# The head of a spectral and gated-MLP kernel: x and the first DFT blocks on two DMA queues, mod's first rows read from PSUM

## The chip, the cores and the metric

The kernel runs on one core of a Trainium2 chip. TensorE (PE in the profile; PEld is its weight load) multiplies matrices, VectorE (DVE), ScalarE (ACT) and GpSimd (POOL) work elementwise, and SyncE (SP) issues most of the transfers from HBM. The metric is the device time of one execution in microseconds; lower is better. All times in this text are microseconds unless they say ns.

## The reference

```python
mod = (_silu(c) @ w_mod).reshape(c.shape[0], 6, 1, -1)
sa, ca, ga, sb, cb, gb = (mod[:, 0], mod[:, 1], mod[:, 2], mod[:, 3], mod[:, 4], mod[:, 5])
h = _layernorm(x, axis=-1) * (1 + ca) + sa
x = x + ga * _A_ref(h, A_dft_seq_re, A_dft_seq_im, A_dft_hid_re, A_dft_hid_im)
h = _layernorm(x, axis=-1) * (1 + cb) + sb
x = x + gb * _B_ref(h, B_w_in, B_w_sp, B_b_sp, B_w_out)
```

x is 2048 x 512, `c` is 1 x 512 and `w_mod` 512 x 3072, all float32. `_A_ref` is the real part of a DFT along both axes: `y = Cr @ (h @ Hr.T) - Ci @ (h @ Hi.T)`, where Cr and Ci are the 2048 x 2048 DFT matrices. `_B_ref` is a gated MLP with a 2048 x 2048 spatial weight. The change touches only what happens before the first DFT products.

## The kernel before

The rows of x are handled in 16 tiles of 128 rows, s = 0 to 15, loaded in four groups of four (`load_x`, one buffer `x0` to `x3` per group). The group's 128 partitions are filled by four transfers, each to 32 partitions, called quarters here.

*mod.* Each of mod's six rows is needed on all 128 partitions. `load_mod(j)` loads the four 128 x 512 pieces `wm` of row j. `sum_mod_first(j, ...)` (L222) sums them on TensorE: `scb` holds silu(c) spread over 128 columns, so that `scb.T @ wm` gives the row on every partition, in PSUM (`modp`). `sum_mod` (L211) does some of the pieces on VectorE ahead of it, into `wm[0]`, and TensorE then adds that partial sum with a matrix of ones. ScalarE copies `modp` into SBUF (`keep_mod`, L209). Row 1 is the scale (1 is added), row 0 the shift.

*h.* For a tile, `stats_x` takes mean and variance on VectorE (L87, L89) and 1/std on POOL (L91 to L99), `norm_x` normalizes on ScalarE into `xn` (L103), `scale_x` multiplies with mod 1 (L278) and `shift_x` adds mod 0 (L281). Tiles 0 to 2 do the last two on VectorE, tile 3 in two fused steps (`make_x`, L283), tiles 4 to 15 on POOL. `hi_h` and `lo_h` then split the result into a rounded part `hh` (ScalarE, L296) and the rest `hl` (VectorE, L301).

*DFT blocks.* The DFT matrices come in 512 x 512 blocks, `load(b)`, four quarters each, into `stage` (two buffers). A block serves four steps n = 4b to 4b + 3: `prep_hi(n)` transposes a part on VectorE (`t`, L142) and rounds it on ScalarE (`ah`, L165), `prep_lo(n)` subtracts on VectorE (`al`, L174). `mm_a(n)` is step n of the product `gp`: twelve matmuls, for each of four banks hh with ah, hh with al, hl with ah (L79 to L81). For the first group of 512 rows of the DFT, steps 0 to 3 use x tiles 0 to 3, steps 4 to 7 the same tiles with block 1, steps 8 to 15 tiles 4 to 7, and so on.

*Order.* It is written by hand. Each engine runs its instructions in the order of the program. The lines at L535 to L567 are the head; after it, `at(n, f, ...)` hangs work on step n of the loop that calls `prep(n)`, `mm_a(n)` and `run(n)`. `prep(n)` prepares three steps ahead. Transfers use eight completion semaphores in turn (DMAHW0 to DMAHW7 below), over all queues; an issue whose semaphore is still held by an earlier transfer waits for that one to land, and what stands behind it on the issuing engine waits too. `keep_busy(n, k)` (L232) issues n matmuls on constant data whose result is not used.

Of the kernel before, what the change touches and what calls it, by code (L numbers as in the profile page):

```python
# [8 lines left out]
F32 = mybir.dt.float32  # L9
# [10 lines left out]
def fnet_gmlp_kernel(  # L20
# [107 lines left out]
    NE = 4 * len(src)  # L128
    stage, T, AH, AL = {}, {}, {}, {}

    def load_block(tile_, a):
        v = a.rearrange("(b j) (a s) -> a j b s", j=32, a=4)
        for q in range(4):
            nc.sync.dma_start(tile_[32 * q:32 * q + 32], v[q])

    def load(b):
        if b < len(src):
            stage[b] = blocks.tile([P, 16, P], F32, tag="stage", bufs=2, name=f"stage{b}")
            load_block(stage[b], src[b])

    def squares(dst, block, k):
        nc.vector.transpose(dst.rearrange("p (b i) -> p b i", i=32), block[:, :, 32 * k:32 * k + 32])  # L142
# [50 lines left out]
    nc.scalar.activation(sc, ccol, AF.Silu)  # L193
# [3 lines left out]
    for k in range(ND):  # L197
        nc.vector.tensor_scalar(scb[:, k, :], ones, sc[:, k:k + 1], None, op0=ALU.mult)
    wm, mods = {}, {}

    def load_mod(j):
        wm[j] = [SP[-1].tile([P, D], F32, tag=f"wm{k}", bufs=2 if len(SP) == 1 else 1, name=f"wm{j}_{k}") for k in range(ND)]
        for k in range(ND):
            nc.sync.dma_start(wm[j][k], w_mod[k * P:(k + 1) * P, j * D:(j + 1) * D])

    def keep_mod(j, ps, pl, plus_one):
        if j not in mods:
            mods[j] = pl.tile([P, D], F32, name=f"mod{j}")
        nc.scalar.activation(mods[j], ps, AF.Copy, bias=1.0 if plus_one else 0.0)  # L209
# [9 lines left out]
                    d = mods[j] = pl.tile([P, D], F32, name=f"mod{j}")  # L219
                nc.vector.scalar_tensor_tensor(d, w[k], sc[:, k:k + 1], w[0], op0=ALU.mult, op1=ALU.add)  # L220

    def sum_mod_first(j, k, pl, plus_one, summed=0):  # L222

        ps = bank(k, f"modp{j}")
        w = wm.pop(j)
        for m in range(summed, ND):
            nc.tensor.matmul(ps, scb[:, m, :], w[m], start=m == summed, stop=not summed and m == ND - 1)
        if summed:
            nc.tensor.matmul(ps, ones, w[0], start=False, stop=True)
        keep_mod(j, ps, pl, plus_one)  # L230

    def keep_busy(n, k):  # L232

        ps = bank(k, "busyp")
        for _ in range(n):
            nc.tensor.matmul(ps, ones, busy, start=True, stop=True)
# [19 lines left out]

    X, XG, LN, NRM, h_hi, h_lo = {}, {}, {}, {}, {}, {}

    def load_x(g, ks=range(4)):

        if g not in XG:
            XG[g] = spool.tile([P, 4, D], F32, tag="x", bufs=2, name=f"x{g}")
        k0, k1 = ks[0], ks[-1] + 1
        v = x.rearrange("(g a k i) d -> g a i k d", g=NQ, a=4, i=32)
        for a in range(4):
            nc.sync.dma_start(XG[g][32 * a:32 * a + 32, k0:k1, :], v[g, a][:, k0:k1, :])
        for k in ks:
            X[4 * g + k] = XG[g][:, k, :]

    def stats_x(s):  # L270
        NRM[s] = norm([X[s]], "x")
# [7 lines left out]

    def shift_x(s, eng):  # L280
        eng.tensor_tensor(LN[s], LN[s], mods[0], op=ALU.add)  # L281

    def make_x(s):  # L283

        mean, rstd = stats([X[s]], "x")
        LN[s] = spool.tile([P, D], F32, tag="xn", bufs=4, name=f"xn{s}")
        nc.vector.scalar_tensor_tensor(LN[s], X.pop(s), mean, mods[1], op0=ALU.subtract, op1=ALU.mult)
        nc.vector.scalar_tensor_tensor(LN[s], LN[s], rstd, mods[0], op0=ALU.mult, op1=ALU.add)

    def parts_h(s, t):  # L290

# [263 lines left out]
    shift_x(1, nc.vector)  # L555
    hi_h(1)
    lo_h(0)
    shift_x(2, nc.vector)
    lo_h(1)
    prep_hi(0)  # L560
    prep_lo(0)
    hi_h(2)
    prep_hi(1)
    prep_lo(1)
    lo_h(2)
    make_x(3)
    prep_hi(2)  # L567
    at(0, hi_h, 3)
    at(1, lo_h, 3)
    at(1, load_x, 2)  # L570
# [201 lines left out]
```

## Time and profile before

| | |
|---|---|
| Median of 3 runs (lowest to highest) | 1002.75 (1002.17 to 1003.09) |
| Profiled execution, its own time | 1002.38 |
| Span of the profiled execution | 1000.6 |
| Mean granted TensorE clock | 0.997 |
| First matmul of the DFT product, after the span's start | 19.75 |
| TensorE busy in 0 to 25 / 25 to 50 / 50 to 100 / 100 to 400 | 17.11 / 25.00 / 49.64 / 300.00 |

The profile is of one execution; times in it count from the start of the span. A row of the timeline gives start, duration, engine, line, operation, output <- inputs, and in brackets the idle time ahead of it with what ended it. A row of the waits gives total, times and longest. A row of the windows gives, for a stretch, the busy time of each engine with its count of instructions, then the granted clock as a share of full speed (PEclk), the busy share of the DMA engines and GB/s.

### The profile page before, as it was taken

How to read it: one execution, taken by the hardware profiler on the slowest of the kernel's cores; microseconds unless marked ns; L12 is line 12 of the kernel's file. 1: busy time of each engine (PE TensorE's matmuls, PEld its weight loads, DVE VectorE, ACT ScalarE, POOL GpSimd, SP SyncE). 2: the span in 40 equal slices, each digit the busy share in tenths (PEclk: the TensorE clock that was granted, in tenths of full speed). 3: DMA queues.
4: the chain of work that ended last, by engine and by line, in shares of the span. 5: the costliest groups of instructions: out<-in, count | busy, mean ns of one | idle time of the engine just before them, and what ended most of it. 6: DMA issues, size and time to landing. Idle time of an engine off the chain costs nothing.

```text
span 1000.6 us, 11611 instructions
## 1 busy us (share of the span) xinstructions
PE 988.1 (99%) x4350; PEld 818.3 (82%) x4350; DVE 544.0 (54%) x820; ACT 295.6 (30%) x450; POOL 173.1 (17%) x281
## 2 busy tenths in 40 slices
PE   6999999999999999999999999999999999999998
PEld 3878888888888888888888998888888888888886
DVE  6888864786465646547433676565332622262315
ACT  3444531432132323222533665431111111111101
POOL 2576002022210122004311121102000200020001
PEclk8999999999999999999999999999999999999999
DMA  9786761555355344556553132435225222521141
GB/s 246 154 189 139 156 147 53 150 156 147 85 148 104 90 111 110 112 126 163 195 199 116 43 83 45 116 71 148 66 63 158 53 64 64 158 69 48 42 138 43
DMA packets 145961, 114.28 MB, mean 114 GB/s; under 512 B 7024, under 2 KB 125808, under 8 KB 145904
## 3 DMA queue, kind: packets, MB, share of 16 engines
q1 hardware_dynamic: 139296, 93.61, 39.7%
q0 software_dynamic: 6080, 19.93, 5.5%
q8 instruction: 34, 0.56, 0.2%
q14 instruction: 23, 0.19, 0.1%
q10 hardware_dynamic: 528, 0.00, 0.0%
HBM read 93.59 MB, written 19.92 MB: 113 GB/s over the span
## 4 chain that ended last, share of the span: by engine, by line
PE 51%; DVE 1%; ACT 0%; POOL 0%; issue 0%; ACTq 0%; POOLq 0%
PE gw L79 10%; PE gw L80 10%; PE gw L81 10%; PE z2p L80 3%; PE z2p L81 3%; PE z2p L79 3%; PE op L79 2%; PE op L81 2%; PE op L80 2%; PE z1p L79 2%; PE z1p L80 2%; PE z1p L81 2%; DVE x_last L518 0%; DVE al L174 0%; DVE t L142 0%; ACT L414 0%
## 5 line engine op out<-in xcount | busy, mean ns | idle before, releaser
L174 DVE TENSOR_TENSOR al<-t,ah 128x512 fp32r<-128x512 f32 x224 | 163.0, 728 | 271.0 <-PE gw L80 139.5
L165 ACT ACTIVATE ah<-t 128x512 fp32r<-128x512 f32 x224 | 141.5, 632 | 543.6 <-PE gw L81 212.5
L79 PE MATMUL gp<-ah,hh 128*128 128x512 f32 x512 | 200.9, 392 | 3.7 <-ACT ah L165 3.4
L80 PE MATMUL gp<-al,hh 128*128 128x512 f32 x512 | 200.3, 391 | 0.0
L81 PE MATMUL gp<-ah,hl 128*128 128x512 f32 x512 | 200.3, 391 | 0.0
L81 PE MATMUL gw<-ah,zl 128*128 128x512 f32 x448 | 174.3, 389 | 0.0
L80 PE MATMUL gw<-al,zh 128*128 128x512 f32 x448 | 174.3, 389 | 0.0
L79 PE MATMUL gw<-ah,zh 128*128 128x512 f32 x448 | 174.3, 389 | 0.0
L142 DVE STREAM_TRANSPOSE t<-stage 128x512 f32<-128x512 f32 x208 | 146.0, 703 | 2.8
L79 PEld LDWEIGHTS gp<-ah,hh 128*128 128x128 f32 x512 | 96.8, 189 | 25.2 <-ACT ah L165 4.2
L80 PEld LDWEIGHTS gp<-al,hh 128*128 128x128 f32 x512 | 96.7, 189 | 20.9 <-DVE al L174 0.7
L81 PEld LDWEIGHTS gp<-ah,hl 128*128 128x128 f32 x512 | 96.7, 189 | 20.6 <-DVE hl L301 0.5
L81 PEld LDWEIGHTS gw<-ah,zl 128*128 128x128 f32 x448 | 84.1, 188 | 17.6
L79 PEld LDWEIGHTS gw<-ah,zh 128*128 128x128 f32 x448 | 84.1, 188 | 17.4
L80 PEld LDWEIGHTS gw<-al,zh 128*128 128x128 f32 x448 | 84.1, 188 | 17.3
L496 POOL TENSOR_TENSOR u<-u,g 128x512 f32<-128x512 f32 x16 | 21.5, 1341 | 336.1 <-DVE g L494 336.1
L367 POOL DMA_DIRECT2D x_d<-xr x16 | 8.8, 548 | 246.5 <-DVE xr L366 246.5
L79 PE MATMUL yp<-hth,gh 128*128 128x512 f32 x128 | 49.8, 389 | 0.0
L80 PE MATMUL yp<-htl,gh 128*128 128x512 f32 x128 | 49.8, 389 | 0.0
L81 PE MATMUL yp<-hth,gl 128*128 128x512 f32 x128 | 49.8, 389 | 0.0
L80 PE MATMUL z2p<-wil,ah 128*128 128x448 f32 x128 | 46.7, 365 | 0.0
L79 PE MATMUL z2p<-wih,ah 128*128 128x448 f32 x128 | 46.7, 365 | 0.0
(106 smaller groups left out, 1164.9 us busy)
## 6 DMA issues: line engine op xcount, KB each, us to landing
stage<-in_A_dft_seq_re_dram SPq DMA_DIRECT2D x64, 256.0 KB, 4.9
stage<-in_A_dft_seq_im_dram SPq DMA_DIRECT2D x64, 256.0 KB, 4.8
stage<-in_B_w_sp_dram SPq DMA_DIRECT2D x64, 256.0 KB, 4.8
stage<-h_d SPq DMA_DIRECT2D x32, 256.0 KB, 4.8
z_d<-z POOLq DMA_DIRECT2D x28, 256.0 KB, 5.8
u<-z_d SPq DMA_DIRECT2D x4, 1792.0 KB, 8.2
wm<-in_w_mod_dram SPq DMA_DIRECT2D x24, 256.0 KB, 5.3
xr<-in_A_x_dram POOLq DMA_DIRECT2D x16, 256.0 KB, 3.1
```

The source lines that it names most:

```text
L79: nc.tensor.matmul(acc, ah, bh, start=first, stop=False)
L80: nc.tensor.matmul(acc, ah, bl, start=False, stop=False)
L81: nc.tensor.matmul(acc, al, bh, start=False, stop=last)
L142: nc.vector.transpose(dst.rearrange("p (b i) -> p b i", i=32), block[:, :, 32 * k:32 * k + 32])
L165: nc.scalar.activation(AH[n], T[n], AF.Copy)
L174: nc.vector.tensor_tensor(AL[n], T.pop(n), AH[n].bitcast(F32), op=ALU.subtract)
L367: nc.gpsimd.dma_start(x2_d[t][i * P:(i + 1) * P, :], x2)
L496: eng.tensor_tensor(U[t][:, f, :], U[t][:, f, :], g, op=ALU.mult)
```

## The change

The head is written anew:

- `load_x` and `load` take an engine and a list of quarters. Quarters 0 and 1 of x's first group go out on ScalarE's queue, 2 and 3 on SyncE's; for block 0, block 1 and x's second group, 0 and 1 go out on SyncE's and 2 and 3 on ScalarE's. All four tiles of x's first group are loaded at once (three, then one, before), and go through `stats_x` and `norm_x` alike; `make_x` is gone.
- `make_sc` comes after the first issues.
- mod 1 is summed on TensorE first and stays in PSUM; tiles 0 and 1 are scaled from there in a fused step (add 1, multiply) on VectorE. Tiles 2 and 3 are scaled on POOL from ScalarE's copy.
- mod 0 has two of its pieces summed on VectorE instead of three; tiles 0 and 1 are shifted from PSUM.
- Block 0's first part is prepared right behind tile 0. In step 0, four matmuls with hh and ah come first, then four with hl, then four with al.
- The three idle matmuls ahead of gp are gone, the two at the start become three.
- The shift of tile 3 and `lo_h` of tile 2 hang on step 0.

```diff
+    def load(b, eng=nc.sync, qs=range(4)):
         if b < len(src):
-            stage[b] = blocks.tile([P, 16, P], F32, tag="stage", bufs=2, name=f"stage{b}")
-            load_block(stage[b], src[b])
+            if b not in stage:
+                stage[b] = blocks.tile([P, 16, P], F32, tag="stage", bufs=2, name=f"stage{b}")
+            load_block(stage[b], src[b], eng, qs)
...
+    def make_sc():
+        nc.scalar.activation(sc, ccol, AF.Silu)
+        for k in range(ND):
+            nc.vector.tensor_scalar(scb[:, k, :], ones, sc[:, k:k + 1], None, op0=ALU.mult)
...
-    def sum_mod_first(j, k, pl, plus_one, summed=0):
+    def sum_mod_first(j, k, summed=0):
 
         ps = bank(k, f"modp{j}")
         w = wm.pop(j)
+        if summed:
+            nc.tensor.matmul(ps, scb[:, summed, :], w[summed], start=True, stop=False)
+            nc.tensor.matmul(ps, ones, w[0], start=False, stop=False)
+            summed += 1
         for m in range(summed, ND):
-            nc.tensor.matmul(ps, scb[:, m, :], w[m], start=m == summed, stop=not summed and m == ND - 1)
-        if summed:
-            nc.tensor.matmul(ps, ones, w[0], start=False, stop=True)
-        keep_mod(j, ps, pl, plus_one)
+            nc.tensor.matmul(ps, scb[:, m, :], w[m], start=m == 0, stop=m == ND - 1)
+        return ps
...
+        if n == 0:
+            for a, b in ((h_hi[s], ah), (h_lo[s], ah), (h_hi[s], al)):
+                for k in range(ND):
+                    nc.tensor.matmul(GP[t, j, k], a[:, k, :], b, start=a is h_hi[s] and b is ah, stop=False)
+            return
...
-    load_x(0, range(3))
+    load_x(0, nc.scalar, (0, 1))
+    load_x(0, nc.sync, (2, 3))
     load_mod(1)
+    make_sc()
     load_mod(0)
-    load(0)
-    load_x(0, range(3, 4))
-    load(1)
-    load_x(1)
-    keep_busy(2, 5)
-    for s in range(3):
+    load(0, nc.sync, (0, 1))
+    keep_busy(3, 5)
+    mod1 = sum_mod_first(1, 7)
+    for s in range(4):
         stats_x(s)
-    for s in range(3):
-        norm_x(s)
-    sum_mod(0, range(3))
-    sum_mod_first(1, 7, spool, True)
-    sum_mod_first(0, 6, spool, False, 3)
-    keep_busy(3, 5)
-    for s in range(3):
-        scale_x(s)
-    shift_x(0, nc.vector)
+    sum_mod(0, range(2))
+    norm_x(0)
+    norm_x(1)
+    load(0, nc.scalar, (2, 3))
+    norm_x(2)
+    keep_mod(1, mod1, spool, True)
+    norm_x(3)
+    for s in range(2):
+        nc.vector.scalar_tensor_tensor(LN[s], mod1, 1.0, LN[s], op0=ALU.add, op1=ALU.mult)
+        scale_x(s + 2, nc.gpsimd)
+    mod0 = sum_mod_first(0, 6, 2)
+    nc.vector.tensor_tensor(LN[0], LN[0], mod0, op=ALU.add)
     hi_h(0)
...
+    prep_hi(0)
+    load(1, nc.sync, (0, 1))
+    load(1, nc.scalar, (2, 3))
+    lo_h(0)
+    prep_lo(0)
+    nc.vector.tensor_tensor(LN[1], LN[1], mod0, op=ALU.add)
+    keep_mod(0, mod0, spool, False)
+    prep_hi(1)
     hi_h(1)
...
+    prep_lo(1)
+    lo_h(1)
+    load_x(1, nc.sync, (0, 1))
+    load_x(1, nc.scalar, (2, 3))
+    prep_hi(2)
     shift_x(2, nc.vector)
...
     hi_h(2)
...
+    at(0, lo_h, 2)
+    at(0, shift_x, 3, nc.vector)
     at(0, hi_h, 3)
     at(1, lo_h, 3)
     at(1, load_x, 2)
```

How the order moves, at the places that the prediction speaks of. First ScalarE, from x's normalization to the first steps (in brackets the semaphores an instruction waits on; the number in a name's middle is the tile, block or step). Before:

```order
L103 ACTIVATE xn0_185<-x0_115,nmrx_165,rsx_162 128x512 [waits DMAHW3_49,DMAHW2_49,DMAHW4_49,DMAHW1_49,Pool_49]
L103 ACTIVATE xn1_187<-x0_115,nmrx_174,rsx_171 128x512 [waits Pool_49]
L103 ACTIVATE xn2_189<-x0_115,nmrx_183,rsx_180 128x512 [waits Pool_49]
L209 ACTIVATE mod1_199<-modp1_194 128x512 [waits PE_49]
L209 ACTIVATE mod0_204<-modp0_201 128x512 [waits PE_49]
L296 ACTIVATE hh0_214<-xn0_185 128x512 [waits DVE_49]
L296 ACTIVATE hh1_217<-xn1_187 128x512 [waits DVE_49]
L165 ACTIVATE ah0_226<-t0_224 128x512 [waits DVE_49]
```

And with the change:

```order
L134 DMA stage0_136<-in_A_dft_seq_re_dram 32x16x128
L134 DMA stage0_136<-in_A_dft_seq_re_dram 32x16x128 [waits DMAHW7_49]
L103 ACTIVATE xn2_192<-x0_110,nmrx_173,rsx_170 128x512 [waits Pool_49]
L212 ACTIVATE mod1_194<-modp1_143 128x512 [waits PE_49]
L103 ACTIVATE xn3_196<-x0_110,nmrx_182,rsx_179 128x512 [waits Pool_49]
L293 ACTIVATE hh0_207<-xn0_186 128x512 [waits DVE_49]
L166 ACTIVATE ah0_211<-t0_209 128x512 [waits DVE_49]
L134 DMA stage1_213<-in_A_dft_seq_im_dram 32x16x128 [waits DMAHW3_49]
L134 DMA stage1_213<-in_A_dft_seq_im_dram 32x16x128 [waits DMAHW5_49]
L212 ACTIVATE mod0_223<-modp0_202 128x512 [waits DVE_49]
L166 ACTIVATE ah1_227<-t1_225 128x512 [waits DVE_49]
L293 ACTIVATE hh1_229<-xn1_188 128x512
```

The first row stands right behind xn of tile 1. Block 0's quarters 2 and 3, two quarters of block 1 and, behind hh1, two of x's second group are now issued from ScalarE's stream; ah0 comes right behind hh0.

VectorE, from mod's partial sum to step 0. Before:

```order
L278 TENSOR_TENSOR xn0_185<-xn0_185,mod1_199 128x512
L278 TENSOR_TENSOR xn1_187<-xn1_187,mod1_199 128x512
L278 TENSOR_TENSOR xn2_189<-xn2_189,mod1_199 128x512
L281 TENSOR_TENSOR xn0_185<-xn0_185,mod0_204 128x512
L281 TENSOR_TENSOR xn1_187<-xn1_187,mod0_204 128x512
L301 TENSOR_TENSOR hl0_219<-xn0_185,hh0_214 128x512
L281 TENSOR_TENSOR xn2_189<-xn2_189,mod0_204 128x512
L301 TENSOR_TENSOR hl1_222<-xn1_187,hh1_217 128x512
L142 STREAM_TRANSPOSE t0_224<-stage0_136 128x512
L174 TENSOR_TENSOR al0_228<-t0_224,ah0_226 128x512
```

And with the change:

```order
L555 SCALAR_TENSOR_TENSOR xn0_186<-modp1_143,xn0_186 128x512
L555 SCALAR_TENSOR_TENSOR xn1_188<-modp1_143,xn1_188 128x512
L558 TENSOR_TENSOR xn0_186<-xn0_186,modp0_202 128x512
L143 STREAM_TRANSPOSE t0_209<-stage0_136 128x512
L298 TENSOR_TENSOR hl0_218<-xn0_186,hh0_207 128x512
L175 TENSOR_TENSOR al0_220<-t0_209,ah0_211 128x512
L565 TENSOR_TENSOR xn1_188<-xn1_188,modp0_202 128x512
L143 STREAM_TRANSPOSE t1_225<-stage0_136 128x512
L175 TENSOR_TENSOR al1_231<-t1_225,ah1_227 128x512
L298 TENSOR_TENSOR hl1_233<-xn1_188,hh1_229 128x512
```

Three instructions instead of eight stand between mod 1 and the first transpose, and all three read a row of mod from PSUM (`modp`).

More of the change, by code (lines that the diff above doesn't have):

```diff
@@ L129, in fnet_gmlp_kernel, with load_block @@
     stage, T, AH, AL = {}, {}, {}, {}
-    def load_block(tile_, a):
+    def load_block(tile_, a, eng=nc.sync, qs=range(4)):
         v = a.rearrange("(b j) (a s) -> a j b s", j=32, a=4)
-        for q in range(4):
-            nc.sync.dma_start(tile_[32 * q:32 * q + 32], v[q])
-    def load(b):
+        for q in qs:
+            eng.dma_start(tile_[32 * q:32 * q + 32], v[q])
+    def load(b, eng=nc.sync, qs=range(4)):
         if b < len(src):
-            stage[b] = blocks.tile([P, 16, P], F32, tag="stage", bufs=2, name=f"stage{b}")
-            load_block(stage[b], src[b])
+            if b not in stage:
+                stage[b] = blocks.tile([P, 16, P], F32, tag="stage", bufs=2, name=f"stage{b}")
+            load_block(stage[b], src[b], eng, qs)
     def squares(dst, block, k):
@@ L192, in fnet_gmlp_kernel @@
     sc = cpool.tile([P, ND], F32, name="sc")
-    nc.scalar.activation(sc, ccol, AF.Silu)
     scb = spool.tile([P, ND, P], F32, name="scb")
@@ L257, in fnet_gmlp_kernel, with load_x @@
     X, XG, LN, NRM, h_hi, h_lo = {}, {}, {}, {}, {}, {}
-    def load_x(g, ks=range(4)):
+    def load_x(g, eng=nc.sync, qs=range(4)):
         if g not in XG:
             XG[g] = spool.tile([P, 4, D], F32, tag="x", bufs=2, name=f"x{g}")
-        k0, k1 = ks[0], ks[-1] + 1
+            for k in range(4):
+                X[4 * g + k] = XG[g][:, k, :]
         v = x.rearrange("(g a k i) d -> g a i k d", g=NQ, a=4, i=32)
[L265 to L268, printed above, removed]
+        for a in qs:
+            eng.dma_start(XG[g][32 * a:32 * a + 32], v[g, a])
     def stats_x(s):
@@ L281, in shift_x @@
         eng.tensor_tensor(LN[s], LN[s], mods[0], op=ALU.add)
[L283 to L288, printed above, removed]
     def parts_h(s, t):
```

12 lines of the change are left out of this document (removed).

## The prediction

> **What bounds the kernel now.** I read the page first: busy times, then the granted clock.
>
> ```profile
> span 1000.6 us, 11611 instructions
> PE 988.1 (99%) x4350; PEld 818.3 (82%) x4350; DVE 544.0 (54%) x820; ACT 295.6 (30%) x450; POOL 173.1 (17%) x281
> ```
>
> TensorE is busy for 99% of the span, so only time in which it has no matmul, or a slow clock, can be won without removing matmuls. The change removes none of the main ones. So the next view is the list of TensorE's waits, over the whole span (total, times, longest):
>
> ```profile
> PE gp L79 <- ACT ah L165: 3.4, 1, 3.4
> PE modp L227 <- DMA wm<-in_w_mod_dram: 3.0, 2, 1.8
> PE gp L79 <- ACT hh L296: 0.3, 1, 0.3
> ```
>
> The first and third concern the DFT product gp. The timeline places the first, and the windows give the clock around it (the value before the last two is PEclk):
>
> ```profile
> 13.63 2.74 PE L236 MATMUL busyp<-busy,ones 128*128 128x512 f32 x6
> 18.34 0.70 DVE L142 STREAM_TRANSPOSE t<-stage 128x512 f32<-128x512 f32 x1
> 19.07 0.63 ACT L165 ACTIVATE ah<-t 128x512 fp32r<-128x512 f32 x1 [1.98 <-DVE t L142]
> 19.75 0.79 PE L79 MATMUL gp<-ah,hh 128*128 128x512 f32 x1 [3.38 <-ACT ah L165]
> 25.34 0.43 PE L79 MATMUL gp<-ah,hh 128*128 128x512 f32 x1
> 25.61 0.40 PE L80 MATMUL gp<-al,hh 128*128 128x512 f32 x1
> 18.60:25.35 6.75, 5.60 (x13) 4.10 (x14) 4.85 (x9) 1.78 (x3) 1.05 (x2) 0.50 1.14 222
> 25.45:40.00 14.55, 14.55 (x66) 12.01 (x65) 13.16 (x23) 7.17 (x12) 5.47 (x9) 1.00 0.93 188
> ```
>
> Useful work starts at 19.75. Twelve matmuls then run at half clock until 25.34, after which they start about 0.23 apart (0.227 over the stretch). At that rate the twelve need 2.7, so TensorE stands as if it had started at 25.34 - 2.7 = 22.6 at full clock. All that the head can win lies before 22.6.
>
> What lets an earlier start through is shown by the third wait. It is at step 11 of gp, for x tile 7:
>
> ```profile
> 32.23 0.68 DVE L87 BATCH_NORM_STATS2 bstx<-x 128x6 f32<-128x512 f32 x1
> 34.23 0.69 DVE L87 BATCH_NORM_STATS2 bstx<-x 128x6 f32<-128x512 f32 x1
> 36.37 1.82 POOL L278 TENSOR_TENSOR xn<-xn,mod 128x512 f32<-128x512 f32 x1
> 51.11 1.29 POOL L281 TENSOR_TENSOR xn<-xn,mod 128x512 f32<-128x512 f32 x1
> 53.11 0.50 PE L79 MATMUL gp<-ah,hh 128*128 128x512 f32 x1 [0.34 <-ACT hh L296]
> ```
>
> From 36.37 to 52.40 POOL scales and shifts tiles 4 to 7 with hardly a pause; it starts once the statistics of tile 5 (34.23) are through. So the gain is the smaller of two: how much earlier TensorE gets there, and how much earlier VectorE reaches tiles 4 and 5. The second loses nothing to the clock.
>
> **The change, part by part.** *Two queues.* The four x quarters and the DFT quarters go to 32 partitions each, wm goes to 128. GB/s in slices of 0.2 us from 1.8 and from 10.6, and of 0.15 us from 28.0:
>
> ```profile
> GB/s 72 102 389 349 88 280 277 143 287 226 225 225 297 225 236 236 195 195 184 195 266 348 389 410 410 400 420 399 410 389 420 389 430 369 451 369 420 369 430 379
> GB/s 389 320 346 351 341 279 225 200 205 207 200 202 210 225 300 230 213 215 218 205 210 195 236 246 226 179 328 195 223 282 230 310 228 208 220 228 200 205 205 200
> GB/s 65 177 188 113 256 311 348 314 335 348 266 229 201 205 202 195 164 154 177 311 287 260 263 249 222 225 208 205 208 242 202 229 236 218 300 259 219 219 219 232
> ```
>
> x moves at about 220 (2.9 to 5.6), wm at 400 (6.2 on), the blocks at about 210 after a burst at 310 to 350. In mid-block the third row rises to 260 to 311 for a microsecond (from 30.8): the place where quarter 1 hands over to quarter 2. So it is not the engines or the packet size alone that hold a 32-partition transfer to 210. The change sends quarters 0 and 1 on one queue and 2 and 3 on the other, so that handover lasts. I price both queues together at wm's 400 for x and at the burst's 330 for the blocks; the bound the other way is the plateau, 220.
>
> [...]
>
> *x tiles, four at once.* One tile (0.26 MB) more must land first. Rows for this and the next steps:
>
> ```profile
> 0.72 0.47 ACTq L187 DMA_DIRECT2D ccol<-in_c_dram  x1
> 6.44 0.69 DVE L87 BATCH_NORM_STATS2 bstx<-x 128x6 f32<-128x512 f32 x1 [1.24 <-DMA x<-in_A_x_dram]
> 10.04 0.81 ACT L103 ACTIVATE xn<-x,nmrx,rsx 128x512 f32<-128x512 f32 x1 [0.56 <-POOL nmrx L99]
> DMA to landing us min/median/max: 3.1/4.6/7.2
> 27.10 1.90 SPq L134 DMA_DIRECT2D stage<-in_A_dft_seq_re_dram  x4
> ```
>
> SP's data begin near 2.2; ScalarE's two quarters are issued 0.47 later, behind ccol, so near 2.7. Their 0.52 MB at half of 400 take 2.6, and 0.3 passes between data and use (x's slices end near 6.1, its first statistics start at 6.44): x is there at 5.6. At the plateau, half of 220, it is 2.7 + 4.8 + 0.3 = 7.8.
>
> *Quarters 2 and 3 of block 0 wait in ScalarE's stream behind xn of tile 1.* That ends 10.04 + 0.81 - 6.44 = 4.4 after x is there: at 10.0. An issue into an idle queue lands in 3.1 (the minimum above, block 2's first quarter, issued at 27.10); the second quarter adds 0.26 MB / 215 GB/s = 1.2. That is 4.3 alone. At half of 330 both take 3.2 instead of 2.4, so 5.1. I take the middle, 4.7: block 0 complete at 14.7 (bounds 14.3 and 15.1). In the plateau case: 12.2 + 1.9 (3.1 less one quarter) + 4.8 = 18.9.
>
> *The rows of mod from PSUM.* VectorE reads PSUM at SBUF's price, and two VectorE steps go:
>
> ```profile
> L494 DVE TENSOR_TENSOR g<-gw,bs 128x512 f32<-128x512 f32 x28 | 18.6, 681 | 9.9 <-PE gw L81 9.5
> L278 DVE TENSOR_TENSOR xn<-xn,mod 128x512 f32<-128x512 f32 x3 | 1.9, 685 | 1.5 <-ACT mod L209 1.5
> L220 DVE SCALAR_TENSOR_TENSOR wm<-wm,sc,wm 128x512 f32<-128x512 f32 x13 | 9.7, 748 | 0.7 <-DMA wm<-in_w_mod_dram 0.4
> 7.01 3.67 PE L227 MATMUL modp<-wm,scb 128*128 128x512 f32 x8 [1.85 <-DMA wm<-in_w_mod_dram]
> ```
>
> A fused step on modp1 is an L220 (0.75), against an L278 before. mod0 now takes three matmuls of 3.67 / 4 = 0.92 instead of two. 3.1 MB of x and wm at 400 end near 10.2, so mod0's sum ends near 12.2 (its last matmul waits for the last wm), and VectorE has tile 0 shifted near 13.0. That is before 14.7: all of this is hidden behind block 0, by 1.7. Without that cover it would decide, at 13.0. The 2.74 of idle matmuls at 13.63 go (one moves to the front): they hid nothing but the clock.
>
> *From block 0 to tile 4's statistics.* Call block 0's arrival S. Then transpose, ah and first matmul take 19.75 - 18.34 = 1.4. VectorE has twenty instructions from the first transpose to the last before tile 4's statistics. Its pace where it runs back to back is 0.64 (31.02 to 31.66); I use 0.65:
>
> ```profile
> 31.02 0.71 DVE L142 STREAM_TRANSPOSE t<-stage 128x512 f32<-128x512 f32 x1
> 31.66 0.65 DVE L174 TENSOR_TENSOR al<-t,ah 128x512 fp32r<-128x512 f32 x1
> 41.71 1.38 DVE L174 TENSOR_TENSOR al<-t,ah 128x512 fp32r<-128x512 f32 x1
> ```
>
> 20 x 0.65 = 13.0: S + 13.0 against 32.23. The 41.71 row is an al beside a running POOL; the change lets POOL scale tiles 2 and 3 at just this time, so I add 0.5 (bounds 0 and two such stretchings, 1.4). Gain = 32.23 - 13.5 - S = 18.7 - S. With S = 14.7: 4.0.
>
> *TensorE's side.* First matmul at 16.1. Its wait since mod0 is 3.9, as long as the one that halved the clock before (3.38), so I let the clock be halved for a full 6.8 as before: 3.4 lost, as if started at 19.5. That is 22.6 - 19.5 = 3.1 earlier, and the waits of step 11 (0.34, and some 0.4 for hl behind it) vanish: 3.6 to 3.8. With a shorter spell of half clock the POOL side binds, at 4.0. I take **3.8**.
>
> *ScalarE's six block and x issues* cost 0.47 each (the ccol row). I count them at nothing where ScalarE waits for VectorE anyway; if uncovered, the four behind the first ah cost 1.9. *The new order of step 0's matmuls* (four with hh and ah, then hl, then al) only lets them start before hl and al exist; their number is the same.
>
> **Sum.** The profiled execution took 1002.38, its span 1000.6, so 1.8 lie around it and stay. 1002.4 - 3.8 = 998.6. That execution is 0.4 below the median of the runs, 1002.75; against the median I forecast **998.9**. The forecast's own range: S at 13.0 (block early, VectorE decides) gives 5.7, S at 15.8 gives 2.9: 997.1 to 999.9.
>
> **Rivals.**
> 1. *The second queue brings no rate.* Both share 220. S = 18.9, gain -0.2: 1003.0. For it: 16 shared engines, with the DMA share at 1.14 already in the window before. Against it: the rise at 30.8, and wm's 400.
> 2. *ScalarE pays for the issues.* The four uncovered, 1.9 off: 1000.8. For it: ah, hh and the issues stand in one stream, and some issues wait for an earlier transfer to land. Against it: ScalarE was busy for 1.78 of 6.75 us at that place.
> 3. *Slower: TensorE's idle stretch outgrows the clock.* With the second set of idle matmuls gone, a late block 0 leaves TensorE without work from mod0 to the first gp, and the full 6.8 of half clock fall on gp. Before, 5.6 of them did. This turns into a loss once 1.4 + S + 3.4 is later than 22.6, from S = 17.8 on; at S = 18.9 it is 1.1 later: 1003.9.
>
> [...]
>
> **How the numbers follow.** Forecast 0.65, rival 1 0.15, rival 2 0.11, rival 3 0.09. The range goes from 996.8 (S below 13, left out with 0.05) to 1003.2, which holds rival 1 and leaves most of rival 3 out. This kernel's runs tell 0.2%, 2 us, from no change. Faster by more than that (below 1000.75): the forecast and half of rival 2, 0.70. Within: rival 1, the rest of rival 2, part of rival 3: 0.23. Slower (above 1004.75): rival 3 with a still later block, 0.07.
>
> **What would show it.** x's first statistics near 5.6 (right) or 7.8 (rival 1); slices near 400 before 5; the first transpose near 14.7 and the first gp near 16.1; tile 4's statistics near 28.2; the PEclk of 0.50 after 15; no wait, or a smaller one, at step 11. A ScalarE issue that waits over 1 us after the first ah is rival 2. The forecast is wrong if block 0 lands after 16, if VectorE's twenty instructions take over 15, or if a new wait of TensorE of over 1 us appears after step 3.

## The result, and the profile after

The change made the kernel slower by a little: 1003.63 us (median of 12 runs, 1003.00 to 1004.53) against 1002.22 (12 runs, 1001.96 to 1003.09) of the kernel before on the same chips. The ratio is 1.0014, with a 95% interval of 1.0005 to 1.0023. The forecast was a gain of 3.8. The profiled execution took 1004.44, near the upper end of its runs; its span was 1002.7, 2.1 more than the span before.

The page of the changed kernel:

```profile
span 1002.7 us, 11598 instructions
PE 989.5 (99%) x4348; PEld 818.7 (82%) x4348; DVE 543.3 (54%) x817; ACT 296.2 (30%) x451; POOL 175.4 (17%) x284
```

TensorE has two matmuls fewer and is busy 1.4 longer, since the sums of mod ran at half clock (shown below). Its list of waits (total, times, longest) has the rest:

```profile
PE gp L321 <- ACT ah L166: 4.4, 1, 4.4
PE modp L234 <- DMA wm<-in_w_mod_dram: 2.6, 2, 2.0
...
PE gp L79 <- ACT hh L293: 0.7, 1, 0.7
```

The wait before the first gp was 3.4 and is 4.4 now, and the one at step 11 was 0.3 and is 0.7. The timeline places them (start, duration, engine; SPq and ACTq are the two engines' DMA issues):

```profile
1.22 1.01 ACTq L272 DMA_DIRECT2D x<-in_A_x_dram  x2
1.64 7.23 SPq L207 DMA_DIRECT2D wm<-in_w_mod_dram  x8
...
10.00 0.70 DVE L87 BATCH_NORM_STATS2 bstx<-x 128x6 f32<-128x512 f32 x1 [4.25 <-DMA x<-in_A_x_dram]
10.25 1.56 SPq L134 DMA_DIRECT2D stage<-in_A_dft_seq_re_dram  x2
...
10.37 5.46 PE L234 MATMUL modp<-wm,scb 128*128 128x512 f32 x6 [0.58 <-DMA wm<-in_w_mod_dram]
...
12.09 0.93 SPq L134 DMA_DIRECT2D stage<-in_A_dft_seq_im_dram  x2
...
13.76 0.81 ACT L103 ACTIVATE xn<-x,nmrx,rsx 128x512 f32<-128x512 f32 x1 [0.71 <-POOL nmrx L99]
13.77 0.86 ACTq L134 DMA_DIRECT2D stage<-in_A_dft_seq_re_dram  x2
...
16.27 0.58 ACT L212 ACTIVATE mod<-modp 128x512 f32<-128x512 f32 x1
16.88 1.29 DVE L555 SCALAR_TENSOR_TENSOR xn<-modp,xn 128x512 f32<-128x512 f32 x2 [2.41 <-ACT mod L212]
18.76 0.69 DVE L558 TENSOR_TENSOR xn<-xn,modp 128x512 f32<-128x512 f32 x1 [0.60 <-PE modp L234]
...
21.67 0.71 DVE L143 STREAM_TRANSPOSE t<-stage 128x512 f32<-128x512 f32 x1 [2.23 <-DMA stage<-in_A_dft_seq_re_dram]
22.42 0.63 ACT L166 ACTIVATE ah<-t 128x512 fp32r<-128x512 f32 x1 [2.31 <-DVE t L143]
23.10 2.04 PE L321 MATMUL gp<-ah,hh 128*128 128x512 f32 x4 [4.38 <-ACT ah L166]
...
34.81 0.68 DVE L87 BATCH_NORM_STATS2 bstx<-x 128x6 f32<-128x512 f32 x1
...
53.57 1.30 POOL L285 TENSOR_TENSOR xn<-xn,mod 128x512 f32<-128x512 f32 x1
...
55.59 0.50 PE L79 MATMUL gp<-ah,hh 128*128 128x512 f32 x1 [0.69 <-ACT hh L293]
```

Read it backwards. The first gp comes 1.4 after the first transpose, which has waited 2.2 for block 0. Tile 4's statistics follow the transpose by 13.1, and step 11 follows them by 20.8 (20.9 before). So what sets the end is block 0: it is complete at 21.6, where 14.7 was forecast and 16.5 was the time before. The clock did not make gp worse. The windows (the value before the last two is PEclk) show 3.41 at half clock on gp, where before there were 5.6 (19.75 to 25.4). The sums of mod ran at half clock from 9.51 to 16.34; VectorE, which waits for them, was still ready 2.2 ahead of block 0:

```profile
9.51:16.34 6.83, 6.25 (x8) 2.52 (x8) 4.28 (x10) 2.42 (x4) 4.45 (x11) 0.50 1.13 322
16.34:23.17 6.83, 2.45 (x7) 0.83 (x5) 3.35 (x6) 2.56 (x5) 2.85 (x4) 1.00 0.97 196
23.17:26.58 3.41, 3.41 (x8) 2.70 (x9) 2.71 (x5) 1.75 (x3) 0.00 (x0) 0.50 1.04 210
26.60:41.00 14.40, 14.40 (x65) 11.92 (x64) 13.66 (x25) 7.25 (x11) 3.98 (x8) 1.00 0.97 201
```

Why block 0 is late is seen in the view of the DMA queues from 14 to 17 (rate in 40 slices; packets, MB and the packets' time as a share of the 16 engines; issues):

```profile
GB/s 205 157 191 198 218 198 225 219 205 225 198 225 232 205 205 212 218 218 198 198 205 205 205 205 212 212 198 198 212 212 198 205 239 198 232 205 219 225 212 225
...
q1 hardware_dynamic: 1264, 0.63, 123.9%
issues: line engine op xcount, KB each, median us to landing
stage<-in_A_dft_seq_re_dram ACTq DMA_DIRECT2D x2, 256.0 KB, 7.1
```

q1 is SyncE's queue, q10 ScalarE's. ScalarE issues block 0's quarters 2 and 3 at 13.8 and 14.1, yet up to 17 its queue moves nothing: no q10 stands in the answer. SyncE has four quarters issued earlier (block 0's 0 and 1 and block 1's 0 and 1), and these go first, at 210. From the DMA records, the moments at which each piece was issued and had landed:

```
piece                 issued   landed
x q2, q3       SP      0.7 1.2   3.7  5.7
x q0           ACT     1.2       7.3
wm1 first      SP      1.6       8.5
x q1           ACT     1.8       9.9
wm, last of 8  SP      8.5      14.8
block 0 q0,q1  SP     10.3 11.5 15.8 17.0
block 1 q0,q1  SP     12.1 12.7 18.2 19.3
block 0 q2,q3  ACT    13.8 14.1 20.6 21.6
```

The pieces land in the order of their issue, as if there were one queue. In the other runs that holds with few exceptions: in e2, below, a quarter that ScalarE issued at 8.3 landed at 15.4, behind a piece of wm that SyncE issued at 8.8 (14.9).

### The profile page after: what moved, and what is told of

Read it like the earlier page. It is cut to its first block, busy times and chain, and to the rows that moved or that the text cites. A ratio compares the mean times of both kernels' runs of the same rounds, so it can differ in the third digit from the quotient of the medians.

```text
span 1002.7 us, 11598 instructions
## 1 busy us (share of the span) xinstructions
PE 989.5 (99%) x4348; PEld 818.7 (82%) x4348; DVE 543.3 (54%) x817; ACT 296.2 (30%) x451; POOL 175.4 (17%) x284
## 4 chain that ended last, share of the span: by engine, by line
PE 94%; DMA 2%; POOL 2%; DVE 1%; issue 0%; ACT 0%; ACTq 0%; DVEq 0%
PE gp L79 11%; PE gp L81 11%; PE gp L80 11%; PE gw L80 10%; PE gw L79 10%; PE gw L81 10%; PE yp L79 3%; PE yp L81 3%; PE yp L80 3%; PE z2p L81 3%; PE z2p L80 3%; PE z2p L79 3%; PE z1p L79 3%; PE z1p L80 3%; PE z1p L81 3%; PE op L79 2%
## 5 line engine op out<-in xcount | busy, mean ns | idle before, releaser
L79 PE MATMUL gp<-ah,hh 128*128 128x512 f32 x508 | 198.1, 390 | 0.7 <-ACT hh L293 0.7
L81 PE MATMUL gp<-ah,hl 128*128 128x512 f32 x508 | 197.8, 389 | 0.0
L80 PE MATMUL gp<-al,hh 128*128 128x512 f32 x508 | 197.6, 389 | 0.0
L79 PEld LDWEIGHTS gp<-ah,hh 128*128 128x128 f32 x508 | 95.4, 188 | 20.9 <-ACT hh L293 1.1
L81 PEld LDWEIGHTS gp<-ah,hl 128*128 128x128 f32 x508 | 95.4, 188 | 20.3 <-DVE hl L298 0.5
```

What stands on the lines that cost most here:

```text
L79: nc.tensor.matmul(acc, ah, bh, start=first, stop=False)
L80: nc.tensor.matmul(acc, ah, bl, start=False, stop=False)
L81: nc.tensor.matmul(acc, al, bh, start=False, stop=last)
```

## The experiments

Theories at the outset. A: transfers of both queues are served in the order of their issue, at the rate of one queue. B: the queues are served in turn, and each loses. C: the new order of the computation is slower by itself. Later, within A: H, neighbours in the line overlap when they write to different halves of the 128 partitions; F, the partitions don't matter. "Before" stands for the kernel before, run on the same chip. All moments in us:

```
kernel   x     wm    block 0  first  tile 4  step  time     ratio to before
         there there there    gp     stats   11    median   (95%)
before    6.3  11.8  16.5     19.75  32.23   53.11 1002.22
after     9.9  14.8  21.6     23.10  34.81   55.59 1003.63  1.0014 (1.0005-1.0023)
e1        8.0  13.4  18.1     19.96  31.67   52.41 1001.20  0.9979 (0.9970-0.9989)
e2        8.8  16.2  18.4     19.88  31.59   51.92 1001.20  0.9985 (0.9976-0.9994)
e3        9.1  14.4  19.0     20.50  32.70   53.81 1001.62  0.9988 (0.9977-0.9998)
e4        8.1  13.7  19.0     20.56  32.27   53.37 1002.33  0.9995 (0.9985-1.0004)
e5        7.7  12.9  16.8     18.20  29.91   50.66 1000.09  0.9979 (0.9970-0.9989)
e6        6.7  13.5  21.2     22.66  34.37   55.12 1004.05  one run
e7        8.0  13.5  17.9     19.34  31.05   52.10 1000.69  0.9985 (0.9975-0.9994)
e8        8.1  19.6  16.1     24.70  35.07   55.82 1004.17  1.0014 (1.0005-1.0024)
e9        6.7  12.7  17.1     18.82  30.53   51.27 1000.57  0.9978 (0.9968-0.9988)
e10       6.1  11.8  16.0     19.10  31.83   52.53 1002.32  0.9995 (0.9985-1.0004)
e11       6.9  13.0  18.4     20.06  31.78   52.54 1001.37  0.9988 (0.9978-0.9998)
e12       8.1  13.7  18.1     19.56  31.27   52.02 1000.56  0.9981 (0.9972-0.9990)
e13       7.8  13.2  17.0     18.40  30.10   50.87 1000.17  0.9978 (0.9969-0.9987)
e14       7.6  13.1  16.6     18.02  28.41   49.71  999.29  0.9968 (0.9956-0.9981)
```

The first three columns and block 0's moments in the text are landings by the DMA records; step 11 is its first matmul. The moments are those of one profiled execution of each kernel. In before and e10 x is three tiles a quarter, in all others four. A ratio is that of the comparison over all its runs, not the quotient of the two medians. The before of each chip had medians of 1002.64 (e1 to e4), 1002.38 (e5 to e8), 1002.37 (e9 to e11) and 1002.57 (e12 to e14).

**e1, all from one queue.** The changed kernel with every `nc.scalar` of its loads turned back:

```
-    load_x(0, nc.scalar, (0, 1))
+    load_x(0, nc.sync, (0, 1))
...
-    load(0, nc.scalar, (2, 3))
+    load(0, nc.sync, (2, 3))
```

and the same for block 1 and x1.

> The changed kernel with all its ScalarE transfers issued from SyncE at the same places of the program; the computing order stays the changed one. Theory A (transfers of both queues are served in the order of their issue, at the rate of one; the head lost because ScalarE issues block 0's second half late, behind half of block 1): x's first group is complete near 7.3 instead of 9.9, block 0 near 18 instead of 21.5, the first gp matmul near 19.4 instead of 23.1, tile 4's statistics near 31.2 instead of 34.8; the time 3 to 3.6 us below the changed kernel's 1003.6, that is about 1 us below the kernel before. Theory B (both queues are served in turn, each at half the rate): x near 7.3 too, block 0 near 18. Theory C (the new computing order itself is slower, the queues do not matter): first gp matmul and time within 1 us of the changed kernel's.

The timeline of e1:

```profile
8.12 0.69 DVE L87 BATCH_NORM_STATS2 bstx<-x 128x6 f32<-128x512 f32 x1 [2.43 <-DMA x<-in_A_x_dram]
...
18.54 0.70 DVE L143 STREAM_TRANSPOSE t<-stage 128x512 f32<-128x512 f32 x1
...
19.96 1.21 PE L321 MATMUL gp<-ah,hh 128*128 128x512 f32 x4 [2.06 <-ACT ah L166]
...
31.67 0.69 DVE L87 BATCH_NORM_STATS2 bstx<-x 128x6 f32<-128x512 f32 x1
```

With one queue less, x is there 1.9 earlier and block 0 3.4 earlier, and the kernel is faster than before (ratio 0.9979). That takes away theory C: the rest of the change gains, and the issues from ScalarE are what loses. A and B expected the same here, so e1 does not tell them apart. Tile 4's statistics stand 13.1 behind the first transpose again.

**e2, block 0's second half issued early.** ScalarE issues it right behind SyncE's half in the program, ahead of its normalizations:

```
     load(0, nc.sync, (0, 1))
+    load(0, nc.scalar, (2, 3))
```

> The changed kernel with block 0's quarters 2 and 3 issued from ScalarE right behind silu(c), ahead of x's normalization; two queues as in the changed kernel. Theory A: they land in the order of issue among wm's pieces, ahead of SyncE's quarters of block 0 and of block 1; block 0 complete near 19.2 (its last quarter is then SyncE's second), 2.4 us earlier than the changed kernel's 21.5, since only block 1's two quarters no longer stand ahead; the time 1.5 to 2.4 us below the changed kernel's. mod's pieces come 1 to 2.4 us later. Theory B: the quarters of the two queues overlap and block 0 is complete at 17 or earlier. Theory C: no change of the time over 1 us.

The quarters are issued at 4.5 and 8.3 and land among wm's pieces, at 11.9 and 15.4, so wm is complete only at 16.2. Block 0 is complete at 18.4, as with one queue; A expected 19.2, B 17 or earlier. Here the early issue changed who goes first and won nothing over e1: block 0 stands 0.3 behind its 18.1, wm 2.8 behind its 13.4.

**e3, block 1 out of the way.** Blocks 1 and x1 go wholly to ScalarE's queue, behind block 0's second half:

```
-    load(1, nc.sync, (0, 1))
+    load(1, nc.scalar, (0, 1))
...
-    load_x(1, nc.sync, (0, 1))
+    load_x(1, nc.scalar, (0, 1))
```

> The changed kernel with block 1 and x's second group issued whole from ScalarE, behind the first ah and hh of tile 1, so that SyncE has nothing queued behind its half of block 0; block 0's quarters 2 and 3 are issued from ScalarE where the changed kernel does it. Theory A: block 0 complete near 19.2, first transpose near 19.3 and first gp near 20.7 (23.1 in the changed kernel), with the issue of quarters 2 and 3 still near 13.8. Theory B and a theory that the late issue alone is the cause: block 0 complete near 21.5 as before. The time itself is held back by ScalarE waiting on its own issues, so it tells little: 1001 to 1004.

Block 0's quarters 2 and 3 are issued at 12.9 and 13.3 and land at 18.0 and 19.0, right behind 0 and 1. From quarter 1's landing to the last it takes 2.2 (16.7 to 19.0), in the changed kernel 4.6 (17.0 to 21.6): the two quarters of block 1 that stood between cost 2.4. Block 0 at 19.0 is A's 19.2 and not B's 21.5; the issue itself came 0.8 earlier too.

**e4, only x from one queue.** Here `load_x(0, nc.sync, (0, 1))` alone replaces ScalarE's.

> The changed kernel with x's first group alone moved to SyncE's queue (quarters 0 to 3, ahead of wm); blocks as in the changed kernel. Theory A: x complete near 7.3 instead of 9.9, mod 1's last piece near 9.9, mod 0's last near 12.4 (14.75 in the changed kernel), block 0 near 19.9 instead of 21.5; the time about 1.6 us below the changed kernel's. If x's share of two queues does not matter: x still near 9.9 and the time within 0.7 us of the changed kernel's.

x is there at 8.1 instead of 9.9, ScalarE comes to block 0's issues earlier (12.0), and one quarter of block 1 instead of two is ahead. Block 0 is complete at 19.0 (19.9 was expected), and the time is as before. Both losses, x's and block 1's, are real, and they feed each other.

**e5 and e13, quarters in another order, beside e1's again (e12).** All from SyncE, with `(0, 2, 1, 3)` in place of `(0, 1)` and `(2, 3)` for x, blocks 0 and 1 and x1.

> The change with every first-stage transfer on SyncE's queue, as in e1_one_queue, but the quarters of x, of blocks 0 and 1 and of x1 in the order 0, 2, 1, 3, so that neighbours in the queue write to different halves of the 128 partitions. [...] Theory F (transfers go one behind the other in the order of their issue, whatever the partitions): x at 8.0, block 0 at 18.1, quarters 1.1 to 1.2 us apart, the time is that of e1, 1001.2.

> e1_one_queue once more (every first-stage transfer from SyncE's queue, quarters in the order 0, 1, 2, 3), beside e13 on one chip. Both theories: 1001.2, block 0 near 18, tile 4's statistics 31.0 to 31.7.

> e5_alternate once more (the same with quarters in the order 0, 2, 1, 3). Theory H (neighbours to different halves overlap): block 0 near 16.8 and tile 4's statistics near 29.9 again, the time 0.7 to 1.3 below e12. Theory F (order does not matter, e5's earlier block was chance): block 0 within 0.5 of e12's and the time within 0.5 of it.

From 14 to 18 both kernels move block 0 and 1. The queue view of e12 (order 0, 1, 2, 3):

```profile
GB/s 215 215 220 189 220 200 231 236 312 271 271 261 261 220 215 236 200 220 225 205 220 205 205 205 210 195 210 205 210 205 230 266 323 287 230 246 251 200 225 220
...
q1 hardware_dynamic: 1847, 0.92, 124.5%
```

And of e13 (order 0, 2, 1, 3):

```profile
GB/s 282 292 312 348 307 261 210 225 220 205 302 287 323 343 312 246 220 220 215 225 302 297 323 338 302 230 200 230 225 236 287 312 328 343 297 200 225 220 210 277
...
q1 hardware_dynamic: 2164, 1.07, 122.5%
```

In e12 the rate is mostly 195 to 236, with two rises to 312 and 323, near 14.8 and 17.2, where the queue goes over from one half of the partitions to the other. In e13 such a rise of half a microsecond stands at every quarter. The mean goes from 229 to 268, the same share of the engines' time moves more, and block 0 is there 1.1 earlier, as H said. The time follows less: 1000.17 against 1000.56, 0.4 with runs that overlap (999.31 to 1001.02 and 1000.21 to 1001.23). That is under the 0.7 to 1.3 that H expected, so in the time the two can't be told apart.

**e10, the same order in the kernel before.** The loops over quarters of x and of all blocks run over `(0, 2, 1, 3)`.

> The kernel before, unchanged but for the order of the quarters of every x group and every DFT block: 0, 2, 1, 3. Theory H (neighbours in one queue overlap when they write to different halves): block 0 is complete near 15.6 instead of 16.5, block 1 near 20.8 instead of 22.4; before's own first transpose at 18.34 waited for VectorE and not for block 0, so its first gp stays near 19.7 and the time falls by at most 0.5, 1002. Theory F: landings as before, 1002.4.

Block 0 is 0.5 earlier, block 1 1.4 (20.95 for 22.36), as H said; the time is that of before. Here VectorE's chain, not the block, is ahead of the first transpose. The first gp, expected to stay near 19.7, came at 19.10, because VectorE's chain began 0.65 earlier in this execution (its first step with mod 1 at 12.68 for 13.33).

**e6, x's halves really side by side.** In the changed kernel c's small load, which ScalarE issued first, goes behind its x quarters.

> The change with the small load of c on ScalarE's queue moved behind its two x quarters, so that both queues issue x at the same moment (0.7 and 1.2) and quarters 0 and 2, 1 and 3 go side by side, with no piece of wm between. Theory H (two queues to two halves run side by side at 400): x complete near 5.6. Theory A (the two queues share what one queue has): x complete near 8.0 as on one queue, and wm's pieces after it as in e1; block 0 still behind half of block 1, so first gp near 22 to 23 and the time 1002 to 1003.6.

Both queues now issue at 0.7 and 1.2, and x is there at 6.7, between H's 5.6 and A's 8.0: nearer to the forecast's 5.6 than any other version with four tiles, but for e9 with the same 6.7. From 2.2 to 5 the two queues move 331, in the changed kernel 221. So A is not the whole of it: issued in the same moments, two queues to two halves moved x faster. But c lands at 8.4, and VectorE, which must make scb ahead of the statistics, begins these only at 9.5. Block 0 waits behind half of block 1 as in the changed kernel; so does the time.

**e9, x side by side, the rest as e5,** with c's load on GpSimd's queue.

> e5_alternate with x's first group on both queues side by side (quarters 2 and 3 from SyncE, 0 and 1 from ScalarE, issued at the same two moments), c's small load moved to GpSimd's queue. If pairs on two queues move as in e6: x complete near 6.7 instead of e5's 7.7, wm and block 0 follow 0.5 to 1 earlier (block 0 near 16), first gp near 17.5, the time 0.3 to 0.8 below e5's 1000.1. If c's load is late from GpSimd's queue, or a second queue gives nothing over alternating on one: x at 7.7, first gp at 18.2 or later, the time is e5's or above.

The start of e9:

```profile
7.63 0.20 ACT L200 ACTIVATE sc<-ccol 128x4 f32<-128x4 f32 x1 [4.70 <-DMA ccol<-in_c_dram]
7.96 0.88 DVE L202 TENSOR_SCALAR scb<-ones,sc 128x128 f32<-128x128 f32 x4 [6.57 <-ACT sc L200]
...
8.74 0.69 DVE L87 BATCH_NORM_STATS2 bstx<-x 128x6 f32<-128x512 f32 x1
```

x is there 1.0 earlier than in e5, but c is late from this queue too and the statistics begin 0.9 later. wm is complete only 0.2 earlier: of the gain 0.6 is left at wm's first piece (7.5 for 8.1) and 0.2 at its last. From 2.2 to 5 e9 moves 324 and e5 235, but in e5 the rate falls to 55 from 3.0 to 3.5, while 274 packets move on the queue that c uses and 16 on SyncE's. So part of x's gain may be that c no longer stands between; that was not tried.

Block 0 comes later than in e5, at 17.1 for 16.8, though wm was earlier. Its quarters, in e13's order from one queue, land 1.1 apart, and from 14 to 18 the rate is 236, where the same order gives 268 to 289 in e5, e10, e13 and e14. Why it gained so little here is not known. The gain of 0.3 to 0.8 that was expected for pairs did not come: the time is e5's within half a microsecond, and above it.

**e11, the change as it was meant.** c from GpSimd, and ScalarE's two quarters of block 0 behind xn of tile 0.

> The change with c's load on GpSimd's queue (so that x's halves go side by side) and block 0's quarters 2 and 3 issued by ScalarE behind xn of tile 0 instead of tile 1, so that they stand in time beside SyncE's quarters 0 and 1 and ahead of block 1. If two queues to two halves run side by side once they are issued side by side: x near 6.7, block 0 near 16, first gp near 17.5, tile 4's statistics near 29.5, the time 999.5 to 1000.5. If they only share: x near 8, block 0 near 18.2, first gp near 20, the time near 1001.2 as e1. If ScalarE's issues come late all the same, block 0 lands behind block 1's first quarters and the time is 1002 or more.

They are issued at 11.3 and 11.7, behind one quarter of block 1 (10.5) and 1.5 behind SyncE's second (9.8). They land at 17.8 and 18.4, behind that quarter. From 14.3 to 15.7, when both queues have packets under way, they move 233 together. x is there at 6.9, as the first case expected; block 0 and the time (1001.37) are those of the second, and the place behind a quarter of block 1 is that of the third. Whether two queues would carry block 0 faster if both halves were issued in the same moments was not tried.

**e7, the clock.** e1 with `keep_busy(3, 5)` put back behind mod 0's sum.

> e1_one_queue with the three idle matmuls before the first gp put back. If the clock decides (rival 3): TensorE's idle stretch before gp shrinks from 2.5 us to under 1, less of gp falls on the half clock, and the time is 0.5 to 1.7 below e1. If VectorE's and POOL's chain to tiles 4 to 7 decides: tile 4's statistics near 31.7 as in e1, the wait at step 11 grows by what TensorE gains, and the time is e1's 1001.2 within 0.5.

The windows around the first gp (19.34) and the first two waits of TensorE behind 15:

```profile
13.00:22.00 9.00, 7.31 (x23) 3.88 (x21) 5.15 (x9) 4.68 (x8) 4.00 (x7) 1.00 1.23 230
```

```profile
PE gp L321 <- ACT ah L166: 1.7, 1, 1.7
PE gp L79 <- ACT hh L293: 1.5, 1, 1.5
```

gp runs at full clock from the start, and step 11 comes at 52.10, where e12, with 3.0 of half clock on gp, has 52.02. What the clock gave stands as waiting time at step 11 (1.5 for 0.9). So the half clock on gp does not decide here; the chain over VectorE and POOL does. The median lies 0.5 below e1's, at the edge of both expectations, but e1 ran on another chip; e12, the same kernel as e1 on this chip, has 1000.56 for 1000.69. Since e2 has no half clock on gp either, without the idle matmuls, the full clock need not be their doing.

**e8, block 0 ahead of wm0,** with two sub-blocks transposed and split while wm0 is under way.

```
     make_sc()
+    load(0, nc.sync)
     load_mod(0)
-    load(0, nc.sync, (0, 1))
```

> e1_one_queue with block 0 in the queue ahead of wm0, and the first two sub-blocks transposed and split on VectorE before mod0's rows are needed. If what decides is when VectorE gets through its twenty instructions: first transpose near 14.5, first gp near 20.5 (mod0 comes last, wm0 lands near 18), tile 4's statistics 2 to 4 us earlier than e1's 31.7 and no wait at step 11; the time is 0.5 to 1.5 below e1, near 1000. If the bytes before the first gp decide alone (x, wm1, wm0 and block 0 are needed in any order): first gp 0.5 to 1 later than e1's 19.96, and the time is 1001.2 to 1002.2.

Its timeline:

```profile
16.24 0.71 DVE L143 STREAM_TRANSPOSE t<-stage 128x512 f32<-128x512 f32 x1
...
23.30 0.69 DVE L562 TENSOR_TENSOR xn<-xn,modp 128x512 f32<-128x512 f32 x1 [1.14 <-PE modp L234]
24.02 0.63 ACT L293 ACTIVATE hh<-xn 128x512 fp32r<-128x512 f32 x1 [1.20 <-DVE xn L562]
24.70 1.19 PE L321 MATMUL gp<-ah,hh 128*128 128x512 f32 x4 [1.44 <-ACT hh L293]
```

Both expectations fall. wm0 last costs far more than block 0 last: from its landing (19.6) to gp there are mod 0's matmuls at half clock, the shift and hh, 5.1 together, where from block 0 it is 1.4. Of the 5.1 some 1.8 is the half clock that fell there in this execution (these matmuls take 3.7 here, 1.9 at full clock in e5). VectorE stands still for mod 0's sum and has 16 of its instructions ahead of tile 4's statistics still to do at 23.30, so these come at 35.07.

**e14, tile 4's statistics earlier.** e13 with the list of steps at which VectorE takes them `[2, 3, 4, 6, 8, 11, ...` for `[3, 4, 5, 7, 9, 11, ...`.

> e13_alternate_again with tile 4's to 8's statistics one step earlier in VectorE's order (x1 lands near 24.3, their first use is at 29.9). If POOL's chain behind these statistics sets the end: they start near 27.5, POOL's last step of tile 7 comes 1 to 2 earlier, the 0.6 of wait at step 11 goes, and the time is 0.3 to 1.5 below e13. If TensorE or VectorE decides instead: the steps of TensorE slip because the sub-blocks' al come later, and the time is e13's or above.

The first row is e13's, at step 11:

```profile
50.87 0.50 PE L79 MATMUL gp<-ah,hh 128*128 128x512 f32 x1 [0.66 <-ACT hh L293]
```

In e14 tile 4's statistics, and all that TensorE's list of waits has between 15 and 62:

```profile
28.41 0.69 DVE L87 BATCH_NORM_STATS2 bstx<-x 128x6 f32<-128x512 f32 x1
```

```profile
PE gp L321 <- ACT ah L166: 3.4, 1, 3.4
```

The wait at step 11 is gone, that step comes 1.2 earlier (0.4 of it because gp began at 18.02 instead of 18.40 in that run), and the median is 0.9 lower. With 999.29 this is the fastest version of the study, 3.3 below before.

## Why the prediction was wrong

It failed in the step "Two queues": it priced both queues together at 400 for x and 330 for the blocks, as if ScalarE's quarters went beside SyncE's. They went behind them, and block 0 was complete at 21.6 instead of 14.7. The sign it had named, block 0 after 16, came.

1. **x complete at 5.6, bound 7.8: 9.9.** Both pairs of quarters were priced at wm's 400 together, because they would go side by side. They did not: c's load put ScalarE's first x quarter 0.5 behind SyncE's, so SyncE's two quarters, both in one half of the partitions, went first (landed at 3.7 and 5.7, ScalarE's at 7.3 and 9.9), and one of wm's pieces (8.5) came in ahead of the last. From 2.2 to 8 the two queues together moved:

```profile
DMA packets 1216, 1.27 MB, mean 219 GB/s; under 512 B 597, under 2 KB 597, under 8 KB 1216
...
q1 hardware_dynamic: 428, 0.78, 52.9%
q10 hardware_dynamic: 788, 0.49, 41.5%
```

That is the plateau, 219, on the mean (in it a fall to 59 from 3.0 to 3.5, while c's small packets move). Even the bound of 7.8 counted x's bytes alone, not wm's that stand between them. Issued at the same moments, with c behind, x was there at 6.7 (e6).

2. **Block 0 complete at S = 14.7 (bounds 14.3 and 15.1; plateau case 18.9): 21.6.** Quarters 2 and 3 were priced as if ScalarE's queue were idle ("alone"). Nothing else was under way on it, but four of SyncE's quarters were issued ahead, and from 14 to 17 SyncE's queue alone moved (0.63 MB on q1, no packet on q10). The plateau case counted block 0's own bytes and left out block 1's two quarters. Of the 6.9 by which S was missed, 3.8 is the issue, at 13.8 instead of 10.0, since x was late (from x to the issue it took 3.9, priced at 4.4). The other 3.1 is the way from issue to landing, 7.8 instead of 4.7; e3 shows 2.4 of it to be block 1's. The queue was also fuller than priced: wm was complete at 14.8, where 10.2 was worked out from 400 GB/s from the start.

3. **What the row at 30.8 meant.** The rise to 311 was read as two halves in parallel, to be had for as long as two queues last. e12 and e13 show that the rise is there, at each handover between the halves, and that it can be had in a single queue by the order of the quarters: 268 for 229. In e9 the order gave less (236). Two queues to two halves went faster only for x in e6, e9 and e11 (complete at 6.7, 6.7 and 6.9, from one queue at 7.6 to 8.1), where both were issued in the same moments; for block 0, issued 1.5 apart in e11, they did not (233 together).

4. **From S on the working held.** First gp S + 1.4: measured 1.5. Tile 4's statistics S + 13.0 and 0.5 for POOL: measured 13.3, with twenty instructions as counted. With S = 21.6 the formula, gain = 18.7 - S, gives a loss of 2.9; the statistics came 2.6 later, step 11 2.5 later, and the span lost 2.1. That VectorE's and POOL's chain hands S on to step 11 is borne out by e7 and e14, and over all 16 kernels: step 11 stands 20.3 to 21.3 behind tile 4's statistics, and from step 11 to the end of the profiled execution it is 948.6 to 949.3.

5. **VectorE ready at 13.0, hidden by 1.7.** It was ready at 19.5, hidden by 2.2. Part of this is x. Part is the clock: mod 1's sum, at half clock, ended at 15.8 (10.37 + 5.46), 4.4 behind its last piece (11.5); in e5, at full clock, it ended 1.9 behind. Part is a wait that was not in the sum: the fused steps on modp1 (16.88) begin as ScalarE's copy out of the same bank ends (16.85), though modp1 was complete by 15.8 and xn of both tiles by 14.6. In e5 this wait is 2.3 (from 12.4 to 14.7). In e1, e2, e8, e9 and e10 VectorE, not block 0, is what the first transpose waits for.

6. **Rivals.** Rival 1, no rate from the second queue, was right in its main point for the changed kernel and too mild in its price, a loss of 0.2 for a measured 1.4, for it left out block 1. Its 220 is near the 219 that both queues moved together from 2.2 to 8; x in e6 (331 from 2.2 to 5) speaks against it in part. Rival 2 did not occur as told: ScalarE's first ah waited for VectorE, not for issues. Rival 3's clock did not outgrow: 3.4 of half clock on gp instead of 6.8. That was luck, for 5.6 fell on it in e3 and none in e2. The forecast put its 6.8 down to the wait ahead of gp; that such a wait brings the half clock no run shows: behind the same wait of 2.06, half clock fell on gp in e1 (four matmuls in 1.91) and none in e2 (1.08). That two transfers issued by two engines would go to both halves at once was the prediction's own step from the rise at 30.8, and that step failed for block 0. Why quarters of 32 partitions kept to 205 to 230, where wm to 128 went at 402 (before, from 6 to 10.6), no run shows.

## What to carry to other kernels

Here a second issuing queue gained rate only where both halves were issued in the same moments (x in e6 and e9: 331 and 324 from 2.2 to 5, for 221 in the changed kernel; in e11 x was complete at 6.9, for 9.9), and no time even then (1004.05, 1000.57 and 1001.37, for 1000.09 in e5). Otherwise the pieces of all queues went, with few exceptions, as one line in the order of their issue (block 0's last quarter, issued at 14.1 behind block 1's two of 12.1 and 12.7, landed at 21.6 behind their 18.2 and 19.3): count them so, and ask of a transfer that is split over two engines what the other engine will have issued ahead of its second half. If transfers cover only some of the partitions, try neighbours of different halves behind each other in one queue before reaching for a second queue; the landings came earlier by it, the time hardly (block 0 by 1.1 and the median by 0.4 in e13 beside e12). Of the inputs that a first product needs, let that one come last which has the shortest path from its landing to the product (1.4 from block 0, 5.1 from wm0 in e8). And follow a change at the head to the step that waits last: here step 11 behind tile 4's statistics, which e14 moved from 30.10 to 28.41 for the lowest time of all, 999.29.

## What the runs showed of the hardware that was not expected

- In the changed kernel a queue with work stood still while another queue's earlier transfers moved: ScalarE's, with 0.5 MB issued by 14.1, moved nothing until 17 (no packet in the queue view from 14 to 17, where SyncE's moved 0.63 MB). It is not strict: in e11 both queues had packets under way from 14.3 to 15.7, at 233 together.
- Quarters of 32 partitions moved at 205 to 230 behind a neighbour of the same half, and at 300 to 340 for some half a microsecond behind one of the other half, at nearly the same packets' share of the engines' time (124.5% and 122.5%). With quarters in turn from both halves the mean from 14 to 18 was 268 to 289 in four kernels and 236 in e9; what sets e9 apart is open.
- A copy by ScalarE and a step by VectorE that read the same PSUM bank came one behind the other (16.27 to 16.85, then 16.88). By the trace the wait stands in the program: VectorE's step waits on the semaphore that ScalarE's copy raises. What the chip would do without it was not tried.
- TensorE's half clock came in stretches of 3.41 and 6.83 that begin at another phase in each execution (18.57 to 25.40 before, with gp from 19.75; 23.17 to 26.58 after; none on gp in e2, e7 and e8). On gp it moved little where step 11 waited for POOL's chain: with none of it in e7 and 3.0 in e12, step 11 came within 0.1.
